# Norming the last batch's rows one stage sooner in VectorE's order, ahead of the sums of MLP features

## The chip, the cores and the metric

The kernel runs on one core of one Trainium2 chip. Its time is what the device takes for one execution, in microseconds (us). TensorE (PE in the profile) does the matrix products, with its weight loads listed apart (PEld); VectorE (DVE) and ScalarE (ACT) do elementwise work and empty PSUM, the memory that TensorE writes to; GpSimd (POOL) does some elementwise work, and SyncE (SP) issues most transfers.

## The reference

Two blocks follow each other: a delta-rule attention over 4 batches, 8 heads, 768 positions and 48 dimensions, and a Fourier mixing block with an MLP over rows of 384. All is float32. The part that the change touches is the last one:

```
u   = x + real(fft(fft(x, axis=1), axis=2))
un  = (u - mean(u)) / sqrt(var(u) + 1e-6)        # per row
ch  = maximum(un @ w_ch1, 0.0) @ w_ch2           # 384 -> 1536 -> 384
out = u + ch
```

## The kernel before, in words

The work goes batch by batch. While the attention of one batch runs, the MLP of the batch before is advanced beside it, piece by piece: each part of the program is a Python generator, and a hand-written order (`period`, and the loop at lines 1396 to 1419) says which generator issues its next piece. The scheduler keeps to this order on every engine, so each engine gets its instructions in just the order in which they are written. The last batch has no attention beside its MLP: after its Fourier stage the generator `mlp(3)` is run to its end alone (`drain(side)`, line 1419). The first two of its pieces, the norming and the transposing of its first rows, are issued during its Fourier stage (line 1416).

The 768 rows of a batch are 6 tiles of 128 rows, and the MLP takes them in 3 groups of two tiles (called pairs 0, 1 and 2 in what follows). The last batch uses these steps for a pair g:

- `normed_of(g)`, line 919: two VectorE instructions norm the two row tiles into two buffers `un`. There are just two such buffers, so the next pair's norming needs the transposes of this one to be over.
- `turned(g)`, lines 929 and 930: TensorE transposes each tile in three blocks of 128 x 128 into PSUM (`ptr`), and ScalarE copies it to `unT`. `ptr` shares its two PSUM buffers (tag `post`) with the results `ph` of the first layer.
- `first_of(g)`, lines 941 to 953: the first layer, 12 feature blocks of 128, each three products `ph` that ScalarE takes through the ReLU into `hT`. (A float32 product is two instructions on TensorE, so a block shows as 6 of them, a pair as 72.)
- The last batch's second layer saves one product in eight with sums made beforehand: of the blocks of hT's 2 x 2 division (`rows_joint`, lines 975 to 978: four VectorE instructions each time that two more blocks are ready, three times in a pair, the last after the last feature block), and of the second weights (`weights_joint`, line 966: four VectorE instructions, once, written during pair 0's first layer).
- `second_joint(g)`, lines 989 to 1007: seven groups of products. The first two (`pa`, `pc`) need hT and the weights themselves, the others the sums. After a group VectorE adds it to the rows (line 1000), and finished rows are sent out. The fifth group adds to the first one's PSUM bank.

Before the change the norming of pair g + 1 (for g = 0) or of pair g + 2 stands in the order right ahead of its transposes, that is behind all of a first layer's pieces, and so, on VectorE, behind the last `rows_joint` of that layer.

Of the kernel before, what the change touches and what calls it, by code (L numbers as in the profile page):

```python
# [64 lines left out]
def kernel(  # L65
# [15 lines left out]
    NC = NL  # L81
# [9 lines left out]
    GT = 2  # L91
# [8 lines left out]
    def ps_pair():  # L100
        return ps.tile([128, 2, 512], F32, tag="pair", bufs=2, name="pair")

    def ps_one():
        return ps.tile([128, 512], F32, tag="one", bufs=2, name="one")

    def ps_post(shape, name):
        return ps.tile(shape, F32, tag="post", bufs=2, name=name)

    def mm(o, lhsT, rhs, start, stop=True):
        nc.tensor.matmul(o, lhsT=lhsT, rhs=rhs, start=start, stop=stop, skip_group_check=True)  # L110

    def tr(o, src, start):
        nc.tensor.matmul(o, lhsT=src, rhs=ident[0:src.shape[0], 0:src.shape[0]],  # L113
                         is_transpose=True, start=start, stop=True, skip_group_check=True)
# [790 lines left out]
    def mlp(b):  # L905
# [8 lines left out]
        def normed_of(g):  # L914

            mv, rstd = norms[g]
            un[g] = [wk.tile([128, DM], F32, tag="un", bufs=2, name="un") for _ in range(GT)]
            for tt in range(GT):
                nc.vector.tensor_scalar(un[g][tt], x[:, GT * g + tt, :], mv[:, tt, 0:1],
                                        rstd[:, tt:tt + 1], op0=ALU.subtract, op1=ALU.mult)  # L920
            yield

        def turned(g):
            rows = un[g]
            un[g] = wk.tile([128, KD, GT * 128], F32, tag="unT", bufs=2, name="unT")
            for tt in range(GT):
                pt = ps_post([128, KD, 128], "ptr")
                for dt in range(KD):
                    tr(pt[:, dt, :], rows[tt][:, 128 * dt:128 * dt + 128], dt == 0)
                nc.scalar.activation(un[g][:, :, 128 * tt:128 * tt + 128], pt, ACT.Copy)  # L930
            yield

        def first_of(g):
            hT = hs[g] = wk.tile([128, KF, GT * 128], F32, tag="big", bufs=2, name="hT")
            for fc in range(KF):
                wide = b == 0 and g == 0 and fc % 4 < 2
                if wide and fc % 2 == 0:
                    both = ps_pair()[:, :, 0:GT * 128]
                ph = both[:, fc % 2] if wide else ps_post([128, GT * 128], "ph")
                for dt in range(KD):  # L940
                    mm(ph, w1[:, dt, 128 * fc:128 * fc + 128], un[g][:, dt, :], dt == 0,
                       dt == KD - 1)
                if not wide:
                    nc.scalar.activation(hT[:, fc, :], ph, ACT.Relu)  # L944
                elif fc % 2:
                    nc.scalar.activation(hT[:, fc - 1:fc + 1, :], both, ACT.Relu)
                if b == 0 and g == 0 and fc == 5:
                    drain(normed_of(1))
                if last:
                    if g == 0:  # L950
                        weights_joint(fc)
                    if fc > kf and fc % 2:
                        rows_joint(g, fc - 1 - kf)
                yield
# [3 lines left out]
        def weights_joint(fc):  # L958
            if fc == 0:
                joint.append(wk.tile([128, 2, kf, n2], F32, tag="O", name="joint0"))  # L960
                joint.append(wk.tile([128, 2, kf, n2], F32, tag="x", bufs=2, name="joint1"))
            t1, t2, t3, t4 = (joint[i // 2][:, i % 2] for i in range(4))
            w11, w12, w21, w22 = (w2[:, h, c] for h in (lower, upper) for c in (left, right))
            for o, p, m in {1: ((t1, w12, w11),), 3: ((t2, w22, t1),), 5: ((t3, w22, w12),),
                            7: ((t4, w21, t2),)}.get(fc, ()):
                nc.vector.tensor_tensor(o, p, m, op=ALU.subtract)

        def rows_joint(g, c):

            if c == 0:  # L970
                sums[g] = wk.tile([128, 4, kf, 128], F32, tag="F", name="joint")
            s1, s2, s3, s4 = (sums[g][:, i, c:c + 2, :] for i in range(4))
            a11, a21, a12, a22 = (hs[g][:, k0:k0 + 2, t:t + 128] for k0 in (c, kf + c)
                                  for t in (0, 128))
            nc.vector.tensor_tensor(s1, a21, a22, op=ALU.add)
            nc.vector.tensor_tensor(s2, s1, a11, op=ALU.subtract)
            nc.vector.tensor_tensor(s3, a11, a21, op=ALU.subtract)
            nc.vector.tensor_tensor(s4, a12, s2, op=ALU.subtract)

        def second_joint(g):  # L980
            h, sg = hs[g], sums.pop(g)
            s1, s2, s3, s4 = (sg[:, i] for i in range(4))
            t1, t2, t3, t4 = (joint[i // 2][:, i % 2] for i in range(4))
            pa, pd = ps_pair()[:, 0, 0:n2], ps_pair()[:, 0, 0:n2]
            pc, pe = ps_one()[:, 0:n2], ps_one()[:, 0:n2]
            x0, x1 = x[:, GT * g, :], x[:, GT * g + 1, :]
            x11, x12, x21, x22 = x0[:, left], x0[:, right], x1[:, left], x1[:, right]

            for o, a, w, start, adds in (
                    (pa, h[:, lower, 0:128], w2[:, lower, left], True, (x11,)),  # L990
                    (pc, h[:, upper, 0:128], w2[:, upper, left], True, (x11,)),
                    (pd, s1, t1, True, (x22,)),
                    (pe, s3, t3, True, (x22,)),
                    (pa, s2, t2, False, (x22, x12, x21)),
                    (pd, s4, w2[:, upper, right], False, (x12,)),
                    (pe, h[:, upper, 128:256], t4, False, (x21,))):
                for i in range(kf):
                    mm(o, a[:, i, :], w[:, i, :], start and i == 0, i == kf - 1)
                for v in adds:
                    nc.vector.tensor_tensor(v, v, o, op=ALU.add)  # L1000
                if o is pa and not start:
                    nc.sync.dma_start(out=out_v[b, GT * g + 1][:, right], in_=x22)
                elif o is pd and not start:
                    nc.sync.dma_start(out=out_v[b, GT * g], in_=x0)
                elif o is pe and not start:
                    nc.sync.dma_start(out=out_v[b, GT * g + 1][:, left], in_=x21)
                yield
# [14 lines left out]
        turns = [normed_of(0), turned(0), first_of(0)]  # L1022
# [5 lines left out]
                      second_of(1, 0), turned(2), second_of(1, 1), first_of(2)]  # L1028
        turns += [second_of(2, 0), second_of(2, 1)]
        if last:  # L1030
            turns = [normed_of(0), turned(0), first_of(0), normed_of(1), turned(1)]
            for g in range(NC // GT):
                turns.append(second_joint(g))
                if g + 1 < NC // GT:
                    turns.append(first_of(g + 1))
                if g + 2 < NC // GT:
                    turns += [normed_of(g + 2), turned(g + 2)]
        for t in turns:
            yield from t

# [8 lines left out]
    def drain(gen):  # L1049
        for _ in gen:  # L1050
            pass
# [124 lines left out]
    with tc.manual_schedule(engines=engines):  # L1176
# [155 lines left out]
        g = NL - 1  # L1332
# [28 lines left out]
        advance(w2s)  # L1361
        advance(f, 2)
        side, done = mlp(0), 0
        advance(ms[7])
        convert(1)
# [29 lines left out]
    with tc.manual_schedule(engines=engines):  # L1395
        for b in range(1, B):
            for g in range(max(NL * b, NL + 2), NL * (b + 1)):
                period(g, side)

            advance(side, KEEP - 12)  # L1400
            drain(fold)
            f, then = fourier(b), mlp(b)
            done = 0
            for i in range(4 + NC):
                advance(f)
                advance(side, 12 * (i + 1) // (4 + NC) - done)
                done = 12 * (i + 1) // (4 + NC)
                if inv and NL * (b + 1) % RL == 0:
                    if i < 3:
                        advance(inv, 3)  # L1410
                    elif i == 3:
                        drain(inv)
                    elif not advance(pm):
                        inv = None
                if i in (6, 8):
                    advance(then)
            drain(side)
            side, done = then, 2
        drain(side)
# [30 lines left out]
```

## Time and profile before

| | us |
|---|---|
| median of 3 runs | 740.95 |
| lowest and highest run | 740.39, 744.5 |
| profiled execution | 738.68 |
| its span | 736.9 |
| TensorE busy in the span | 685.5 |
| VectorE busy | 402.6 |
| ScalarE busy | 262.9 |
| GpSimd busy | 79.6 |

The span is the time from the first to the last instruction of one profiled execution; 1.78 us of that execution's time lie around it. A busy time is an engine's instructions added up; TensorE's are pipelined, so a busy TensorE need not be TensorE at its peak, and its granted clock is listed apart, as a share of full speed. The last batch's first layer of pair 0 begins near 636 us in the span, and the last addition to its rows is at 733.7 us. In the timelines an instruction's idle time in brackets is that of its engine just before it, with the instruction that ended it.

### The profile page before, as it was taken

Reading aid. Unit: us, or ns where it says so; the run is one execution under the profiler, and the core shown is the slowest. Engines: PE = TensorE matmul, PEld = TensorE weight load, DVE = VectorE, ACT = ScalarE, POOL = GpSimd, SP = SyncE. Lnnn points to the kernel's source line nnn. Section 1 sums busy time; section 2 is a strip of 40 time slices with the busy share of each in tenths; the row PEclk is TensorE's granted clock in tenths of the full one; section 3 lists DMA queues with packets and bytes.
Section 4 is the critical chain, followed back from the end, with each engine's and each line's share of the span. In section 5 each row is a group of like instructions: output and inputs, shape, how many; then the busy total and the mean of one; then the engine's idle time right before and its main releaser. Section 6 shows DMA issues by size and latency. Waiting matters only on the chain.

```text
span 736.9 us, 23386 instructions
## 1 busy us (share of the span) xinstructions
PE 685.5 (93%) x10284; PEld 545.0 (74%) x10284; DVE 402.6 (55%) x1017; ACT 262.9 (36%) x642; POOL 79.6 (11%) x138
## 2 busy tenths in 40 slices
PE   7877979977999998999999999999999999989898
PEld 4676878756767677778678778777677687779897
DVE  5878887699712899251785246488112332731322
ACT  5544763896324222144323423232232122211120
POOL 8000001120000110131101210120112100100000
PEclk8799989999999999999999999999999999999999
DMA  9942552153123220012222220011210000000000
GB/s 153 225 75 42 124 114 86 24 146 98 24 50 81 49 46 18 12 33 46 46 51 38 49 43 12 12 28 34 43 31 13 24 1 12 12 1 22 0 22 22
DMA packets 109224, 36.12 MB, mean 49 GB/s; under 512 B 101921, under 2 KB 105666, under 8 KB 109122
## 3 DMA queue, kind: packets, MB, share of 16 engines
q1 hardware_dynamic: 107298, 33.86, 21.5%
q8 instruction: 81, 1.33, 0.8%
q0 software_dynamic: 640, 0.43, 0.4%
q10 hardware_dynamic: 1184, 0.33, 0.3%
q14 instruction: 21, 0.17, 0.1%
HBM read 29.88 MB, written 4.72 MB: 47 GB/s over the span
## 4 chain that ended last, share of the span: by engine, by line
PE 79%; DVE 11%; ACT 6%; issue 2%; DMA 1%; ACTq 0%; DVEq 0%; SPq 0%
PE ph L110 22%; PE po L110 19%; PE one L110 18%; PE pair L110 14%; PE one L113 2%; PE ptr L113 2%; PE unread L1189 1%; DVE tmp L446 1%; DVE M L450 1%; DMA C<-in_k_dram 1%; ACT GU L395 1%; PE pf L110 1%; DMA K<-in_k_dram 1%; DVE MT L651 1%; ACT G L385 1%
## 5 line engine op out<-in xcount | busy, mean ns | idle before, releaser
L110 PE MATMUL ph<-unT,w 128*128 128x256 f32 x828 | 197.0, 390 | 0.0
L110 PEld LDWEIGHTS ph<-unT,w 128*128 128x128 f32 x828 | 154.9, 192 | 22.6
L110 PE MATMUL po<-w,hT 128*128 128x384 f32 x432 | 157.4, 497 | 0.0
L944 ACT ACTIVATE hT<-ph 128x256 f32<-128x256 f32 x138 | 52.9, 383 | 159.1 <-PE ph L110 158.2
L110 PEld LDWEIGHTS po<-w,hT 128*128 128x128 f32 x432 | 76.3, 190 | 38.4
L744 DVE TENSOR_TENSOR S<-S,pair 128x192 f32<-128x192 f32 x40 | 13.9, 349 | 72.3 <-PE pair L110 72.3
L110 PEld LDWEIGHTS one<-V,MT 64*64 64x64 f32 x768 | 29.3, 137 | 20.4 <-issue 6.9
L887 DVE TENSOR_TENSOR x<-x,one 128x193 f32<-128x193 f32 x24 | 8.5, 354 | 63.9 <-ACT Q L878 63.9
L110 PE MATMUL one<-V,MT 64*64 64x48 f32 x768 | 34.6, 224 | 5.5 <-DVE V L701 5.3
L450 DVE TENSOR_TENSOR M<-M,tmp 128x31 f32<-128x31 f32 (+15 forms) x93 | 34.6, 372 | 3.2
L446 DVE TENSOR_TENSOR tmp<-A,M 128x31 f32<-128x31 f32 (+15 forms) x93 | 34.0, 366 | 2.3
L701 DVE TENSOR_TENSOR V<-V,pair 128x192 f32<-128x192 f32 x33 | 11.5, 350 | 38.2 <-PE pair L110 34.1
L899 POOL TENSOR_SCALAR rstd<-mv 128x1 f32<-128x1 f32 x24 | 6.9, 286 | 221.7 <-DVE mv L895 221.7
L110 PEld LDWEIGHTS one<-dtab,F 97*128 97x128 f32 (+1 forms) x192 | 25.0, 191 | 7.7 <-ACT KT L320 1.8
L110 PE MATMUL one<-MT,ND 64*64 64x64 f32 x768 | 29.1, 227 | 1.1 <-ACT MT L649 0.7
L320 ACT ACTIVATE QT<-one 128x512 f32<-128x512 f32 x24 | 14.3, 596 | 39.8 <-PE one L113 39.7
L110 PE MATMUL one<-dtab,F 97*128 97x97 f32 (+1 forms) x192 | 26.2, 276 | 2.5 <-ACT KT L320 1.4
L110 PEld LDWEIGHTS one<-MT,ND 64*64 64x64 f32 x768 | 26.6, 142 | 2.5 <-ACT MT L624 1.1
L110 PEld LDWEIGHTS pair<-U,K 64*64 64x64 f32 x704 | 15.3, 135 | 15.7 <-issue 12.5
L566 POOL TENSOR_TENSOR MT<-A,pack 128x512 f32<-128x512 f32 x12 | 12.6, 1053 | 126.8 <-PE one L110 65.3
L711 ACT ACTIVATE U<-one 128x192 f32<-128x192 f32 x36 | 11.9, 331 | 38.4 <-PE one L110 38.4
L110 PE MATMUL pair<-KT 48*32 48x64 f32 (+1 forms) x1152 | 20.8, 237 | 4.6 <-ACT KT L320 3.2
(202 smaller groups left out, 1136.5 us busy)
## 6 DMA issues: line engine op xcount, KB each, us to landing
w<-in_moe_w_ch_dram SPq DMA_DIRECT2D x12, 384.0 KB, 7.3
E<-in_moe_w_ch_dram SPq DMA_DIRECT2D x12, 384.0 KB, 3.2
K<-in_k_dram SPq DMA_DIRECT2D x92, 48.0 KB, 3.1
V<-in_v_dram SPq DMA_DIRECT2D x92, 48.0 KB, 2.3
out_dram<-x SPq DMA_DIRECT2D x21, 192.0 KB, 1.9
C<-in_k_dram SPq DMA_DIRECT2D x18, 192.0 KB, 9.4
Q<-in_q_dram SPq DMA_DIRECT2D x18, 192.0 KB, 3.6
w<-in_q_dram SPq DMA_DIRECT2D x6, 192.0 KB, 7.6
```

The lines of the kernel that those rows point to most:

```text
L110: nc.tensor.matmul(o, lhsT=lhsT, rhs=rhs, start=start, stop=stop, skip_group_check=True)
L113: nc.tensor.matmul(o, lhsT=src, rhs=ident[0:src.shape[0], 0:src.shape[0]], is_transpose=True, start=start, stop=True, skip_group_check=True)
L320: nc.scalar.activation(dst.rearrange("p h j t -> p (h j t)"), pt, ACT.Copy)
L385: nc.scalar.activation(dst[rw], src[rw, :, :, W:C], ACT.Copy)
L446: nc.vector.tensor_tensor(t, A[:, j + 1:W, j:j + 1].broadcast_to([128, n, j + 1]), M[:, j:j + 1, 0:j + 1].broadcast_to([128, n, j + 1]), o ...
L450: nc.vector.tensor_tensor(M[:, j + 1:W, 0:j + 1], M[:, j + 1:W, 0:j + 1], t, op=ALU.add)
L566: nc.gpsimd.tensor_tensor(MT, MTd[:, m8, None, :].broadcast_to([128, 8, 2, W]), m_blk[:, None, :, None].broadcast_to([128, 8, 2, W]), op=A ...
L701: nc.vector.tensor_tensor(R4, R4, pw[:, :, 0:2 * D].rearrange("p a (j e) -> p a j e", e=D), op=ALU.subtract)
L711: nc.scalar.activation(U.rearrange("p j e -> p (j e)"), pu[:, 0:4 * D], ACT.Copy)
L744: nc.vector.tensor_tensor(s1v, s0.rearrange("p h j e -> p h (j e)"), pk, op=ALU.add)
L887: nc.vector.tensor_tensor(near, near, pb[:, 0, 0:MH + 1], op=ALU.add)
L944: nc.scalar.activation(hT[:, fc, :], ph, ACT.Relu)
```

## The change

In the last batch's order of steps, the norming of pair 1 is moved ahead of pair 0's first layer, and the norming of pair 2 ahead of pair 0's second layer. The transposes keep their places. No step is added or left out.

```diff
         if last:
-            turns = [normed_of(0), turned(0), first_of(0), normed_of(1), turned(1)]
+            turns = [normed_of(0), turned(0), normed_of(1), first_of(0), turned(1)]
             for g in range(NC // GT):
+                if g + 2 < NC // GT:
+                    turns.append(normed_of(g + 2))
                 turns.append(second_joint(g))
                 if g + 1 < NC // GT:
                     turns.append(first_of(g + 1))
                 if g + 2 < NC // GT:
-                    turns += [normed_of(g + 2), turned(g + 2)]
+                    turns.append(turned(g + 2))
         for t in turns:
             yield from t
```

## The prediction

> **What bounds the kernel now.** I read first the page's 40 slices of the span (each 18.4 us), to find the stage, then the chain of waits through the end of the span, then TensorE's timeline, last the busy time and clock of each stretch.
>
> ```profile
> PE   7877979977999998999999999999999999989898
> ...
> PEclk8799989999999999999999999999999999999999
> ```
>
> From the tenth slice on TensorE is nearly always busy; the breaks are in the last batch's MLP (slices 36 and 38). The chain of waits runs there through TensorE alone, apart from two detours. The first, in order of time (start, us, what):
>
> ```profile
> 636.15 15.55 PE ph L110 x72
> 651.71 0.02 issue
> 651.73 0.39 ACT hT L944
> 652.12 0.02 issue
> 652.15 0.44 DVE joint L975
> 652.58 0.02 issue
> 652.61 0.42 DVE joint L976
> 653.03 0.34 DVE joint L977
> 653.37 0.34 DVE joint L978
> 653.70 0.40 DVE un L919
> 654.10 0.14 issue
> 654.24 1.51 PE ptr L113 x6
> ```
>
> TensorE ends the first layer of a pair of row tiles, ScalarE takes the last features, VectorE makes four sums of them, only then norms the next pair's rows, and TensorE waits for these to transpose them. The sums are wanted much later. TensorE's timeline (start, busy, instruction; in brackets the idle time before it and who ended it) has the gap, and the next pair's, and the third pair's turn, which has no transposes:
>
> ```profile
> 654.24 1.51 PE L113 MATMUL ptr<-pack,un 128*128 128x128 f32 x6 [2.54 <-DVE un L919]
> 655.54 3.08 PE L110 MATMUL pair<-w,hT 128*128 128x192 f32 x12
> 658.46 2.11 PE L110 MATMUL one<-w,hT 128*128 128x192 f32 x12
> ...
> 688.40 1.51 PE L113 MATMUL ptr<-pack,un 128*128 128x128 f32 x6 [2.54 <-DVE un L919]
> ...
> 719.85 2.11 PE L110 MATMUL pair<-w,hT 128*128 128x192 f32 x12
> 721.79 2.11 PE L110 MATMUL one<-w,hT 128*128 128x192 f32 x12
> ```
>
> The first product after the gap needs 658.46 - 655.54 = 2.92 us from its start to its successor's, while the same twelve instructions need 721.79 - 719.85 = 1.94 us at the third pair. Busy time by stretch says why; the number after POOL's is the granted clock:
>
> ```profile
> 651.70:654.20 2.50, 0.00 (x0) 0.00 (x0) 2.02 (x6) 0.38 (x1) 0.00 (x0) 0.97 0.00 0
> 654.20:658.20 4.00, 3.96 (x17) 4.00 (x18) 0.28 (x1) 0.98 (x2) 0.00 (x0) 0.59 0.01 4
> 658.20:685.80 27.60, 27.60 (x147) 25.45 (x145) 6.05 (x17) 4.23 (x11) 0.00 (x0) 1.00 0.05 15
> ```
>
> Each gap is followed by some 4 us at a mean clock of 0.59 (0.60 after the second). So a gap costs twice: as idle time, and as slow work after it.
>
> [...] (1 - 0.59) x 4.00 = 1.64 us lost, 3.3 us at half rate. [...] an idle time of 2.54 us was enough here. On the other side, gaps of 0.58 us at 482 and 632 us left the clock at 1.00 (stretches 480 to 484 and 629 to 635). [...] the norming at 653.62 has had its inputs since 631.2 us (mean at 630.2, reciprocal root on GpSimd from 630.59, 0.57 us) and stands behind sums that wait for ScalarE.
>
> **The change, part by part.** No instruction is added or removed. The order of TensorE, ScalarE, GpSimd and SyncE is the same in both programs, DMA issues included; only VectorE's differs. The sum is for the profiled execution, 738.68 us with a span of 736.9; it lies 2.27 us below the median of the runs, 740.95 (lowest 740.39), and I take the saving off both.
>
> *Pair 1's norming*, two instructions (0.86 us together), goes ahead of the four weight differences of line 966. Queued behind it on VectorE are those four: they end at 641.94 + 0.86 = 642.8, the first sums can only begin at 646.97, and the first product with a weight difference is due at about 656.5. It waits for pair 0's transposes to leave its buffers, which they did at 632.7, and for the roots, there at 631.2; it can run at 636.75. Cost: nothing, with 4 us of cover; were the cover gone, 0.86 us.
>
> *Pair 1's transposes* then wait for no rows. What is late next is their PSUM: they take the two buffers of the first layer's last two tiles. The first is free before 651 (ScalarE read it from 650.43, 0.39 us), the second when ScalarE ends at 652.12. The last first-layer matmul starts at 651.31 and its successor can follow 0.22 us later (15.55 / 72), at 651.53. Three transposes at 0.135 (the six at 574.58 took until the next matmul at 575.39: 0.81 / 6) bring it to 651.93; a wait until about 652.2 (estimate: 652.12 and the 0.04 to 0.14 us that a release took in this trace), 0.27 us; three more, 652.6. Then the first product, 1.95 us at full clock, and its successor starts at 654.55. Before it started at 658.46. Saved: 3.91 us, of which 2.27 are idle time and 1.64 clock.
>
> *The same at pair 2*: last first-layer matmul at 685.48, so the successor at 685.48 + 3.24 = 688.72, against 692.61: 3.89 us. The shift is in TensorE's own stream, and the chain to the end runs through TensorE without a break, so all of it arrives at the end. **Sum: 7.8 us.** The tail after VectorE's last addition is unchanged.
>
> *Pair 2's norming*, now ahead of the additions of pair 0's second layer, gains a wait: its buffers are those that pair 1's transposes read. These end at 652.6, the sums before it on VectorE at 653.7; no wait. It takes 0.86, to 654.5; behind it stands the addition of the first product, complete at about 654.7. That has time until the product's bank is written again, at about 652.6 + 4 x 1.95 = 660.4. Nothing is lost. *The sums* must be there for the third product, at 652.6 + 3.9 = 656.5; they end at 653.7, so 2.8 us of cover are left. That TensorE can run on over them is shown by the third pair: the first product starts at 719.85 and the sums run beside it until 722.0.
>
> **Bounds.** The unknown is the wait for the second transpose buffer. At nothing the saving is 2 x 4.17 = 8.3; at 0.58 us (what the transposes at 632.13 waited for their only free buffer) it is 7.2. I take 0.27.
>
> **Rivals.**
> 1. *The clock stays slow though the gap is gone* (the slow stretch then belonged to the transposes and not to the idle time). For it: [...] a small gap of 0.27 us remains. Against it: transposes at 574 us with no gap, and at 632 with gaps of 0.58 us, ran at 1.00. It leaves 2 x 2.27 = 4.5 us: 736.4.
> 2. *The stall moves on*: TensorE stops at the third product for the sums or the weight differences, which comes to the same end. For it: the sums still come last on VectorE. Against it: 2.8 us of cover, and the third pair. It eats the gain only if the sums end some 6.7 us later than now; then 741. That the change doesn't do what it says has the same time, but the built order shows the norming moved in both places.
> 3. *Slower: the chip grants less clock to a denser TensorE.* Place: the 75 us from 652 to the end. The gain is gone when the mean clock there falls below 75 / (75 + 7.8) = 0.91, and the kernel is slower by 0.5% below 75 / (75 + 11.5) = 0.87. At 0.85 it costs 75 / 0.85 - 75 = 13.2, less 7.8: 746.4. Against it: from 400 to 600 us TensorE is busy 198.14 of 200 us at a clock of 1.00.
>
> **How the numbers follow.** The likeliest: 740.95 - 7.8 = 733.1 (a profile near 730.9), chance 0.85. Rival 1: 736.4, 0.07. Rival 2: 741, 0.05. Rival 3: 746.4, 0.03. The range goes from 738.68 - 8.3 = 730.4 (the upper bound of the gain, taken off the quickest execution seen) to rival 1's 736.4; outside are rivals 2 and 3, 0.08 together, and what the runs scatter. Half a per cent is 3.7 us, about what a measurement here can tell from no change: faster 0.85 + 0.07 = 0.92, same 0.05, slower 0.03.
>
> **What would show it.** In the profile after: no idle time of TensorE for the normed rows, and under 0.5 us ahead of each pair's second three transposes, ended by ScalarE; a clock of 1.00 in the 4 us after; the first product at 1.95 us in all three pairs; VectorE's norming at about 637 and 654; the addition after it not late. I would be wrong if the clock is near 0.6 after the transposes though no gap is left (rival 1), if TensorE's idle time stands ahead of the third product (rival 2), or if the clock is below 1.00 throughout (rival 3).

## The result and the profile after

| us | before | after |
|---|---|---|
| median of 4 runs each | 742.4 | 733.25 |
| lowest and highest | 740.39, 744.5 | 732.32, 735.5 |
| profiled execution | 738.68 | 732.32 |
| its span | 736.9 | 730.5 |
| first layer of pair 0 begins at | 635.99 | 637.50 |
| from there to the end of the span | 100.91 | 93.00 |

The ratio of the changed kernel to the one before is 0.9881, 95% interval 0.984 to 0.9921: about 1.2% faster. The predicted 733.1 us is 0.15 us from the median, partly by luck: it was a gain of 7.8 us taken off a median of 740.95, and with the fourth run the median of before is 742.4, so that the medians lie 9.15 us apart. The ratio's interval stands for a gain of 5.9 to 11.9 us; the profile below is sharper.

The spans differ by 6.4 us, less than the last stage gains. The last stage began 1.51 us later in the profiled execution of the changed kernel, although both programs are the same up to there; a second profile of the changed kernel has its beginning at 639.03, and in the runs below whose program is the same up to there it lies between 635.42 and 641.70. So single spans scatter by several us ahead of the place that was changed, and the last two rows of the table are the measure to use: the last stage became 100.91 - 93.00 = 7.91 us shorter. (Spans are given to 0.1 us, so such a length is good to about 0.05 us.)

TensorE's timeline of the changed kernel, in the same places as before (start, busy, instruction):

```profile
653.04 1.19 PE L113 MATMUL ptr<-pack,un 128*128 128x128 f32 x6
654.07 2.12 PE L110 MATMUL pair<-w,hT 128*128 128x192 f32 x12
656.02 2.11 PE L110 MATMUL one<-w,hT 128*128 128x192 f32 x12
...
683.26 1.18 PE L113 MATMUL ptr<-pack,un 128*128 128x128 f32 x6
```

The brackets with the idle time for the normed rows are gone in both places. Six transposes last 654.07 - 653.04 = 1.03 us, and the first product 656.02 - 654.07 = 1.95 where it needed 2.92. The 4 us from the transposes on, at pairs 1 and 2 (granted clock after POOL's number):

```profile
653.00:657.00 4.00, 3.85 (x26) 3.57 (x25) 2.66 (x7) 1.31 (x3) 0.00 (x0) 1.00 0.01 4
683.20:687.20 4.00, 3.85 (x26) 3.56 (x24) 1.88 (x5) 1.37 (x3) 0.00 (x0) 1.00 0.00 0
```

The clock is 1.00, where it was 0.59 and 0.60. What is late now is to be read from the chain of waits:

```profile
637.67 15.55 PE ph L110 x72
653.22 0.02 issue
653.24 0.39 ACT hT L944
653.64 0.04 issue
653.68 0.55 PE ptr L113 x3
654.23 1.95 PE pair L110 x12
```

The detour through VectorE's four sums and its norming is gone. What is left is ScalarE's last ReLU, which the second three transposes need, since they are written to the PSUM buffer that it empties. VectorE's own timeline has the moved instructions and what stands behind the second of them:

```profile
638.18 0.86 DVE L919 TENSOR_SCALAR un<-x,mv,rstd 128x384 f32<-128x384 f32 x2
...
655.13 0.86 DVE L919 TENSOR_SCALAR un<-x,mv,rstd 128x384 f32<-128x384 f32 x2
656.22 0.35 DVE L1000 TENSOR_TENSOR x<-x,pair 128x192 f32<-128x192 f32 x1 [0.22 <-PE pair L110]
```

The second norming has no bracket: it did not wait for its buffers. The addition behind it waited for its product (0.22 us, ended by TensorE) and not for the norming.

### The profile page after: what moved, and what is told of

It is laid out like the page before. It is cut to its first block, busy times and chain, and to the rows that moved or that the text cites. A ratio compares the mean times of both kernels' runs of the same rounds, so it can differ in the third digit from the quotient of the medians.

```text
span 730.5 us, 23386 instructions
## 1 busy us (share of the span) xinstructions
PE 684.3 (94%) x10284; PEld 543.5 (74%) x10284; DVE 402.7 (55%) x1017; ACT 263.1 (36%) x642; POOL 79.2 (11%) x138
## 4 chain that ended last, share of the span: by engine, by line
PE 80%; DVE 12%; ACT 6%; issue 2%; DVEq 0%; ACTq 0%
PE ph L110 23%; PE po L110 19%; PE one L110 18%; PE pair L110 13%; PE one L113 3%; PE unread L1191 2%; PE ptr L113 1%; DVE tmp L446 1%; DVE M L450 1%; ACT GU L395 1%; PE pf L110 1%; DVE MT L651 1%; DVE Z L647 1%; ACT G L385 1%; DVE O L299 0%
## 5 line engine op out<-in xcount | busy, mean ns | idle before, releaser
L110 PEld LDWEIGHTS one<-V,MT 64*64 64x64 f32 x768 | 31.1, 143 | 20.5 <-issue 6.9
L110 PE MATMUL one<-V,MT 64*64 64x48 f32 x768 | 36.4, 229 | 5.6 <-DVE V L701 5.3
L711 ACT ACTIVATE U<-one 128x192 f32<-128x192 f32 x36 | 11.9, 331 | 38.4 <-PE one L110 38.4
```

Of the source, the lines that this page charges most:

```text
L711: nc.scalar.activation(U.rearrange("p j e -> p (j e)"), pu[:, 0:4 * D], ACT.Copy)
```

## The experiments

The theory was the prediction's: a norming behind the sums costs TensorE an idle time of 2.3 us more than needed, and the clock that falls on it costs 1.6 us more, in each of two places. Rivals were that the gain sits in one place, that the slow stretch isn't the answer to the idle time, and that the stall only moves on to the sums. All figures called "last stage" below are, as in the table above, from the start of pair 0's first layer to the end of the span in the profiled execution; ratios are to the kernel before, run on the same chip.

**One half of the change at a time.** Pair 1's norming alone:

```diff
-            turns = [normed_of(0), turned(0), first_of(0), normed_of(1), turned(1)]
+            turns = [normed_of(0), turned(0), normed_of(1), first_of(0), turned(1)]
```

> Only pair 1's norming is moved, pair 2's stays behind its sums. Theory (each norming behind the sums costs an idle time of TensorE of 2.3 us and 1.6 us of half clock after it, and the two places are independent): from the last first-layer matmul to the second product 3.2 us at pair 0 instead of 7.15, unchanged 7.1 at pair 1; 3.9 us off the kernel before, ratio about 0.995. Rival (the gain sits in one of the places only, or the other place takes up the first one's gain): 0 or 7.8 us off.

Ratio 0.9957 (0.9941 to 0.9972); last stage 737.4 - 640.27 = 97.13, so 3.78 us less. TensorE's timeline of this kernel shows one place mended and the other as before:

```profile
655.81 1.18 PE L113 MATMUL ptr<-pack,un 128*128 128x128 f32 x6
...
688.74 1.21 PE L113 MATMUL ptr<-pack,un 128*128 128x128 f32 x6 [2.55 <-DVE un L919]
689.74 3.54 PE L110 MATMUL pair<-w,hT 128*128 128x192 f32 x12
```

In the unmended place the mean clock is 0.57 from 688.70 to 692.70, and the slow stretch sits somewhat later than in the kernel before: the transposes take 1.00 us here (689.71 - 688.40 = 1.31 before) and the product 693.11 - 689.74 = 3.37 (692.61 - 689.71 = 2.90 before). Together they are 4.37 against 4.21 us: the loss is about the same, but which instructions bear it differs between the two runs.

Pair 2's norming alone:

```diff
+                if g + 2 < NC // GT:
+                    turns.append(normed_of(g + 2))
                 turns.append(second_joint(g))
...
-                    turns += [normed_of(g + 2), turned(g + 2)]
+                    turns.append(turned(g + 2))
```

> Only pair 2's norming is moved. Theory: 3.9 us off the kernel before as well, at pair 1's turn alone, ratio about 0.995; together with the run that moves pair 1's alone it makes up the whole gain. Rival (one place has it all): 0 or 7.8 us off.

Ratio 0.995 (0.9929 to 0.9972); last stage 734.5 - 637.62 = 96.88, 4.03 us less. The halves make up the whole, 3.78 + 4.03 = 7.81 against 7.91: the gains add up, and the rival that one of them has it all is out.

**Idle time and clock apart.** In the order of before, useless products fill most of each gap. They are read by nobody and go to a free PSUM buffer:

```diff
+        def warmed(n):
+            one = ps_one()
+            for _ in range(n):
+                nc.tensor.matmul(one[:, 0:DM], lhsT=evt[:, 0, 0:128], rhs=evt[:, 0, 0:DM],
+                                 start=True, stop=True, skip_group_check=True)
+            yield
...
-            turns = [normed_of(0), turned(0), first_of(0), normed_of(1), turned(1)]
+            turns = [normed_of(0), turned(0), first_of(0), normed_of(1), warmed(3), turned(1)]
...
-                    turns += [normed_of(g + 2), turned(g + 2)]
+                    turns += [normed_of(g + 2), warmed(3), turned(g + 2)]
```

> The order of before, with three products of a constant table (128x384, read by nobody) put on TensorE ahead of each of the two late pairs of transposes, about 1.95 us of work in each gap of 2.54. Nothing comes sooner: the transposes still wait for the normed rows. Theory (the slow stretch is the clock's answer to the idle time): the clock stays at 1.00, six transposes take 0.8 and the first product 1.95 us, so 1.6 us are saved in each place, 3.3 in all, ratio about 0.9956. Rival (the slowness belongs to the transposes or to the wait on VectorE, not to idleness): the clock stays near 0.6 over these 4 us and nothing is saved.

Ratio 0.9956 (0.9932 to 0.9979); last stage 735.4 - 637.52 = 97.88, 3.03 us less, 1.5 in each place. TensorE's timeline, and the clock of the 4 us from the transposes on:

```profile
653.06 2.10 PE L1025 MATMUL one<-evt 128*128 128x384 f32 x6
655.77 0.91 PE L113 MATMUL ptr<-pack,un 128*128 128x128 f32 x6 [0.61 <-DVE un L919]
656.51 2.12 PE L110 MATMUL pair<-w,hT 128*128 128x192 f32 x12
```

```profile
655.80:659.80 4.00, 4.00 (x27) 3.92 (x28) 0.56 (x2) 0.88 (x2) 0.00 (x0) 1.00 0.01 4
```

The transposes still wait for VectorE's norming, and no useful work begins sooner. Still 3 us came off, since TensorE idled 0.61 us instead of 2.54 and its clock stayed at 1.00. So the slow stretch is the answer to idleness in these two places; it belongs neither to the transposes nor to the wait.

**How long an idle time it takes.** The norming was put between the last four sums, after the first, second or third of them (removed from the order of steps, and written into `rows_joint`):

```diff
             nc.vector.tensor_tensor(s1, a21, a22, op=ALU.add)
+            if c == kf - 2 and g + 1 < NC // GT:
+                drain(normed_of(g + 1))
             nc.vector.tensor_tensor(s2, s1, a11, op=ALU.subtract)
```

> The order of before, but pairs 1 and 2 are normed after the first of the last four sums instead of after the fourth: three sums of 0.34 us go behind the norming, so TensorE's idle time falls from 2.54 to about 1.5 us in both places. Theory (idle time and clock are two costs, and the clock falls only if the idle time is long enough; between 0.6 us, which it bore, and 2.54, which it didn't, the bound isn't known): with the clock at 1.00 after the gap 2.66 us are saved in each place, 5.3 in all, ratio 0.993; with the clock at 0.6 it is 1.0 in each, 2.0 in all, ratio 0.997. Rival (only the idle time counts, the slowness is there whatever its length): 2.0.

> The same with the norming after the third of the last four sums: idle time about 2.2 us. Theory: 2.0 us saved in each place if the clock holds (4.0 in all, ratio 0.9946), 0.34 in each if it falls (0.7 in all, ratio 0.999); where the bound lies between 1.5 and 2.54 us shows in the two runs together. Rival: 0.7.

> The order of before with pairs 1 and 2 normed after the second of the last four sums. The runs so far put idle times at 1.42 us (clock held) and 2.21 us (clock fell) for the first and the third sum; this one should lie between, at about 1.8. It is to narrow the bound: if the clock holds, 0.74 + 1.6 = 2.3 us come off in each place, 4.7 in all, ratio 0.9937; if it falls, 0.74 in each, 1.5 in all, ratio 0.998. [...]

In order of idle time, TensorE's lines at the transposes of pair 1, first after the first sum:

```profile
655.77 0.91 PE L113 MATMUL ptr<-pack,un 128*128 128x128 f32 x6 [1.42 <-DVE un L919]
656.52 2.12 PE L110 MATMUL pair<-w,hT 128*128 128x192 f32 x12
```

after the second:

```profile
657.44 0.91 PE L113 MATMUL ptr<-pack,un 128*128 128x128 f32 x6 [1.88 <-DVE un L919]
658.18 2.12 PE L110 MATMUL pair<-w,hT 128*128 128x192 f32 x12
```

after the third:

```profile
656.52 1.42 PE L113 MATMUL ptr<-pack,un 128*128 128x128 f32 x6 [2.21 <-DVE un L919]
657.73 3.26 PE L110 MATMUL pair<-w,hT 128*128 128x192 f32 x12
```

| norming after | idle time, us | last stage, us | less than before | ratio (95%) |
|---|---|---|---|---|
| sum 1 | 1.42, 1.42 | 734.3 - 638.65 = 95.65 | 5.26 | 0.9906 (0.9873 to 0.9939) |
| sum 2 | 1.88, 1.88 | 736.4 - 639.86 = 96.54 | 4.37 | 0.9948 (0.9928 to 0.9968) |
| sum 3 | 2.21, 2.21 | 739.1 - 638.61 = 100.49 | 0.42 | 0.9979 (0.9958 to 0.9999) |
| sum 4 (before) | 2.54, 2.54 | 736.9 - 635.99 = 100.91 | 0 | 1 |

From the fourth sum to the third 0.33 us less idle time in each place brings 0.42 us in all, less than the 0.66 of idle time itself. From the third to the second the same 0.33 us brings 3.95. There the clock changes from 0.57 over the 4 us behind the gap to 1.00.

The table orders the gaps by their length; it doesn't show that length alone decides. Nor did the clock fall when TensorE stopped. These are two neighbouring stretches of the kernel before (TensorE's busy time first, its clock after POOL's number):

```profile
650.66:654.08 3.42, 1.03 (x5) 0.57 (x3) 2.35 (x8) 0.54 (x2) 0.00 (x0) 1.00 0.00 0
654.08:657.49 3.41, 3.25 (x13) 3.29 (x14) 0.40 (x2) 0.98 (x2) 0.00 (x0) 0.50 0.02 5
```

The clock is still 1.00 through nearly all of the idle time (651.69 to 654.24) and is 0.50 from 654.08 to 657.49. At pair 2 TensorE idles from 685.86 to 688.40, and the clock is 0.50 from 688.21 to 691.62. In both places the idle time was nearly over when the clock fell.

All runs taken together, nine idle times of the last stage were followed by slow work, and they lasted 2.06 to 3.09 us: the two of the kernel before (mean clock 0.59 and 0.60 over the next 4 us), one each with pair 1's and pair 2's norming moved alone (0.57 and 0.62), two with the norming after sum 3 (0.57 in both places), and three in the run with 17 sums below, there read from the times of the products. The six that weren't lasted 0.61, 1.42 and 1.88 us, each length in two places, and the clock behind them stayed at 1.00 for at least the next 3.3 us.

Length isn't the whole answer, though. In the attention stage of the kernel before TensorE idles 1.60 us from 279.03 to 280.63, less than the 1.88 us above, and the clock is 0.50 from 282.02 to 285.44. The changed kernel has the same there: 1.61 us of idle time until 282.16, and a clock of 0.50 from 283.45 to 286.86. The products there are smaller ones in part (64 x 64); whether that is the reason was not tried.

**Has the stall only moved on?** The changed kernel, with the first of the last four sums written several times over, so that VectorE's sums end later and nothing else changes:

```diff
-            nc.vector.tensor_tensor(s1, a21, a22, op=ALU.add)
+            for _ in range(6 if c == kf - 2 else 1):
+                nc.vector.tensor_tensor(s1, a21, a22, op=ALU.add)
```

> The changed kernel with the first of the last four sums written six times instead of once, in all three pairs: VectorE's sums end about 2 us later (5 x 0.4). Theory (the sums have 2.8 us of cover before the third product): nothing is lost, TensorE's stream has no gap, ratio to the kernel before as for the changed kernel, 0.988. Rival (the sums are what the second layer waits for, the stall has only moved): 2 us are lost in each pair, 6 in all, and the change's gain is nearly gone, ratio 0.996.

Ratio 0.9881 (0.9828 to 0.9935); last stage 734.6 - 641.57 = 93.03, the changed kernel's own to 0.03 us. Five more sums on VectorE ahead of the second layer cost nothing. With 17 in place of 6:

> The same with that sum written seventeen times: 16 x 0.34 to 0.46 = 5.4 to 7.4 us later. Theory: the first of the sums is 3.9 us ahead of the third product in pairs 0 and 1 and 2.8 in pair 2, so TensorE now idles 1.5 to 3.5 us there (2.6 to 4.6 in pair 2) within the third product, and where the gap is over 2.5 us the clock falls as well for 1.6 us more: 6 to 16 us slower than the changed kernel, ratio to the kernel before 0.996 to 1.009. Rival (no cover): 16 to 22 us slower than the changed kernel, ratio 1.010 to 1.018.

Ratio 1.008 (1.0052 to 1.0108); last stage 747.8 - 641.7 = 106.1, 13.1 us more than the changed kernel's. TensorE's timeline at pair 0's third product:

```profile
662.16 1.46 PE L110 MATMUL pair<-joint,joint 128*128 128x192 f32 x8
665.69 1.32 PE L110 MATMUL pair<-joint,joint 128*128 128x192 f32 x4 [2.07 <-DVE joint L976]
666.81 3.43 PE L110 MATMUL one<-joint,joint 128*128 128x192 f32 x12
```

It stops inside the third product, as foreseen, and idles 2.07, 2.06 and 3.09 us in the three pairs, 7.2 in all. The work behind these three gaps is slow too, as behind the gaps of the kernel before, and that is most of the remaining 5.9 us: in pair 0 the four instructions behind the gap take 666.81 - 665.69 = 1.12 us where 0.65 would do, and the next product 670.08 - 666.81 = 3.27 where 1.95 would, 1.79 us in all; in pairs 1 and 2 it is as much (1.78 and 1.79), about what the slow clock costs behind the other gaps. The seventeen sums take 7.78 us where one takes 0.43, so 7.35 us of delay brought 2.07 us of idle time in pairs 0 and 1: the cover ahead of this sum, the time by which it is early, is some 5.3 us there and 4.3 in pair 2. So the sums are the next limit, but with cover to spare as they stand.

**What is left.** The second three transposes wait for the last ReLU because they share its PSUM buffers. Here the late transposes get two buffers of another tag:

```diff
-                pt = ps_post([128, KD, 128], "ptr")
+                if last and g:
+                    pt = ps_one()[:, 0:KD * 128].rearrange("p (k t) -> p k t", k=KD)
+                else:
+                    pt = ps_post([128, KD, 128], "ptr")
```

> The changed kernel, with the transposes of pairs 1 and 2 of the last batch put into the two PSUM buffers of another tag, which are free, so that the second three wait for no ReLU. Theory (that wait is all that is left between first layer and second): the six transposes follow the first layer without a break and take 0.8 us instead of 1.03, so 0.2 us come off in each place, 0.4 to 0.5 in all, which only the profile can show; ratio to the kernel before about 0.988. Rival (the first product, whose features the last ReLU doesn't touch, or the second, whose it does, waits in its place): nothing comes off.

Ratio 0.9872 (0.9844 to 0.99); last stage 727.7 - 635.42 = 92.28, 0.72 us less than the changed kernel's: 0.36 in each place, where 0.2 to 0.25 was expected, since unbroken transposes turned out quicker (0.66 us for six) than the 0.8 that had been read off a place among other work. The ratio alone could not show this; the stage does.

The same was then done for the first transposes of batches 1 to 3, which wait 0.58 us for ScalarE in the Fourier stage:

```diff
+                elif b and g == 0:
+                    pt = ps_pair()[:, 0, 0:KD * 128].rearrange("p (k t) -> p k t", k=KD)
```

> The kernel with the late transposes in free PSUM buffers, and besides the first transposes of batches 1 to 3, each of whose second three wait 0.58 us for ScalarE to empty the only free buffer of their tag, put into two buffers of a third tag that is idle in the Fourier stage. Theory (the waits are TensorE's own and nothing else stands behind them): each of the three places takes 0.66 us instead of 1.46, 2.4 us in all, on top of the 0.74 us of the two late places: 3.1 us below the changed kernel, ratio to the kernel before about 0.984. Rival (the Fourier stage's products wait for VectorE instead): no more than the 0.7 us, ratio 0.987.

> The changed kernel once more, beside the two others on the same chip, for the comparison with the version that has the free buffers: ratio to the kernel before 0.988 to 0.990, no idle time of TensorE for normed rows, clock 1.00 after the transposes.

Ratio 0.9843 (0.9818 to 0.9868), beside 0.9891 (0.9873 to 0.9908) for the changed kernel on the same chip; the medians are 730.21 and 733.78, 3.6 us apart, where 3.1 was expected. TensorE's timeline at the first and at the second transposes of the last batch:

```profile
629.56 0.82 PE L113 MATMUL pair<-pack,un 128*128 128x128 f32 x6
630.21 1.03 PE L110 MATMUL one<-dtab,F 97*128 97x97 f32 x8
...
649.23 0.82 PE L113 MATMUL one<-pack,un 128*128 128x128 f32 x6
```

Six transposes run without a break in both. The kernel before needed 632.51 - 631.06 = 1.45 us in the first place and idled 0.58 of them. This version has the lowest ratio of all that were run; its interval overlaps with that of the version before it.

## Why the prediction was right

- *Where the kernel was bound*: right. The chain of waits had a detour through the sums and the norming in two places, and nothing else of the last stage changed when it was taken out.
- *The cost of a gap, idle time and slow clock*: right for these programs, 7.8 us predicted and 7.91 measured in the last stage. Each place was put at 3.9; alone they gave 3.78 and 4.03. The clock's part was put at 1.64 in each place; filling the gaps without ending the waits gave 3.03 / 2 = 1.52, so the mean clock over 4 us overstated it a little, and the idle part is 7.91 / 2 - 1.52 = 2.43, not 2.27. The two errors nearly cancel, which is luck. The prediction also took the slow clock as the sure consequence of a gap. So it was for the 2.54 us that were there, but in the same places gaps of 1.42 and 1.88 us were followed by a clock of 1.00.
- *The transposes' wait for their second buffer*: the mechanism was right (the release came from ScalarE's last ReLU) and the place was sized at 1.07 us in all, with 1.03 measured. Two terms of it were off in opposite directions: the transposes themselves were put at 0.135 us each and are 0.11 (0.66 / 6), and the break for the buffer is thus 1.03 - 0.66 = 0.37 us, not 0.27.
- *The moves costed at nothing*: right. The first norming ran at 638.18, which is 636.67 less the later start of the stage, and the weight differences behind it still ended before the first sums. The second ran at 655.13, without a wait, and the addition behind it waited for TensorE alone. The sums' cover, put at 2.8 us, was tried from both sides: 5 more sums cost nothing, 16 more made TensorE stop. The size was too low: the sum tried had some 5.3 us at pairs 0 and 1. TensorE ran eight of the third product's twelve instructions before it stopped for it, while the prediction counted from the end of all four sums to the start of that product.
- *The rivals*: that the clock stays slow without the gap is refuted by the clock of 1.00 and by the filled gaps. That the stall moves on is refuted as the kernel stands, and shown to come if the sums are made late enough. A clock that falls for a denser TensorE did not show up: over the changed kernel's last stage, 637.5 to 730.5 us, it is 1.00.
- *What the trace of before already showed*: the reading of the 40 slices passed over slice 16 (276 to 295 us, 8 tenths busy). The idle time of 1.60 us at 279.03 lies there, with a clock of 0.50 behind it (282.02 to 285.44). So there was an example of a gap between 0.58 and 2.54 us that was not borne.

What stays open is what decides whether the clock falls. In the last stage nine gaps of 2.06 us or more were followed by slow work and six of 1.88 or less by a clock of 1.00, in this kernel alone; the 1.60 us at 279.03, with a clock of 0.50 behind them, show that length alone doesn't decide. No run moved a gap of one length to another place.

## What to carry to other kernels

A gap of the busiest engine is to be costed with what comes after it: here 2.4 us of avoidable idle time drew a loss of another 1.5 us of half clock behind it, and work that did nothing, put into the gap, brought back the second part alone. Whether a gap draws the slow clock did not go by its length alone here (1.60 us did in the attention stage, 1.88 us did not in the last), so the second part is to be read from the trace of the kernel at hand. Where the trace shows an engine at its work in the order written (here VectorE: the norming had its inputs at 631.2 us and its buffers at 632.7, and ran at 653.62, behind the sums), work whose inputs are ready belongs ahead of work that still waits, if the other engine needs it first; the move is free as long as what is displaced keeps its cover, which can be measured by writing it several times over. When a gap is closed, the next thing to look for is the buffer that its successor shares with what it overtakes.

## What was not expected of the hardware

- The clock fell late. In the kernel before TensorE stopped at 651.69 us, and the clock was 1.00 until 654.08, then 0.50 until 657.49. A slow stretch can even begin after work has begun again: the idle time in the attention stage ended at 280.63 us, and the clock was 0.50 only from 282.02.
- A small difference in idle time decided much in the last stage: between 1.88 and 2.21 us of it in two places the stage grew from 96.54 to 100.49 us. Of these 3.95 us only 2 x 0.33 = 0.66 are the longer idle time; 1.65 us in each place came with the clock, 1.00 behind the gap in the one case and 0.57 over 4 us in the other. The gaps of 2.06 and 2.07 us in the run with 17 sums were followed by slow products as well (3.18 and 3.27 us for 1.95). An idle time of 1.60 us in an earlier stage was followed by a clock of 0.50.
- Shortening the idle time from 2.54 to 2.21 us in two places brought next to nothing, 0.42 us in all. An improvement that stopped there would have been taken for a failure.
- Two profiled executions of one program had the start of the last stage at 637.50 and 639.03 us, and ended it within 0.07 us of the same length (93.00 and 93.07).
